# First heads by selecting matmuls, values in column tiles, and all first loads on one queue

## Chip, cores and metric

The kernel runs on one NeuronCore of a Trainium2 chip. The metric is the device time of one execution in microseconds; the time before is the median of three runs, 556.89 us (555.47 to 558.24).

The engines are named as in the profile: PE is TensorE (PEld its weight loads), DVE is VectorE, ACT is ScalarE, POOL is GpSimd and SP is SyncE, which here only issues DMAs.

## What is computed

Four layers in turn on x of 2048 rows and 640 features: attention with a memory, a feed-forward layer, and both once more with the same weights. Cut to what matters:

```python
def _A_ref(x, wq, wk, wv, wo, beta):
    H, Dh, N, L = 32, 20, 4, 512
    q, k, v = ...            # (x @ w), by head, in N segments of L rows
    phi = lambda t: jnp.where(t > 0, t + 1.0, jnp.exp(t))
    g = _sigmoid(beta).reshape(1, H, 1, 1)
    M, z = 0, 0
    for s in range(N):
        p = _softmax(qs @ ks.T * scale + causal_mask)
        a_dot = p @ vs
        a_mem = (phi(qs) @ M) / (phi(qs) @ z + 1e-06)
        outs.append(g * a_mem + (1.0 - g) * a_dot)
        M = M + phi(ks).T @ vs
        z = z + phi(ks).sum(rows)
    return o @ wo

def _B_ref(x, w1, w2):       # 640 -> 1728 -> 640
    return jnp.maximum(x @ w1, 0) @ w2

x = x + _A_ref(_layernorm(x), wq, wk, wv, wo, beta)
x = x + _B_ref(_layernorm(x), w1, w2)
x = x + _A_ref(_layernorm(x), wq, wk, wv, wo, beta)
x = x + _B_ref(_layernorm(x), w1, w2)
```

All arrays are bfloat16; sums are kept in float32.

## The kernel before

**Tiling and staging.** x stays in SBUF as 16 tiles of 128 rows (`x_sb`). A segment has 512 rows, four tiles; the work goes through eight pairs (a, s): layer pair a = 0, 1, segment s = 0 to 3. For each, the rows are normalised, transposed (`xnT`, or parts of `hT` for the early segments), and q, k (features on partitions, five column blocks c of 128, in `stg`) and v (rows on partitions, `v_aug`) are projected. Heads have 20 features. Scores want four heads on the four quarters of the 128 partitions, at 32 hh; so q and k are brought from the dense layout of `stg` into a buffer `pad`, which holds a pair of head groups z = 0, 1 (a group is four heads) for q and k. As a rule this goes through DRAM: `spill` writes a block of `stg` to `scr`, `fill` reads it back head by head, both on SP's queue.

**Scores, exponentials and values.** For each pair of groups there are five rounds of scores (`scores`, row tiles of PE), ten exponentials of 128 x 1024 on ACT into `PT` (`exps`), causal masks on POOL, and then for each group the product with the values (`apply`). There are two forms of it. `apply_by_token` makes rows the partitions: 40 matmuls with weights from `PT` and 21 columns each, and then the division from PSUM by three DVE instructions into `o_sb` (lines 1360 to 1364). The other form, at line 1308, makes four heads four column tiles of PE: 16 matmuls of 512 to 128 columns; the result, features on partitions, is copied to `otu` (line 1318, DVE or ACT), a pair is transposed by a DMA on SP's queue into `otk` (`turn_pair`), and divided by DVE (`divide`, lines 1394 to 1402). `otu` has one buffer. `BY_TOKEN = G` = 8: all eight groups of segment 0 of the first layer go by token, the other 56 by column tiles.

**The opening.** `loads` issues x tiles 0 and 1 on SP's queue, tiles 2 and 3 and beta on ACT's, and then on SP's the first 256 columns of k's and q's weights, the other 384 of each, v's weights and the four x tiles of segment 1. `warm_pe` gives PE 41 matmuls of 128 columns meanwhile. `first_sums` takes the statistics of tiles 0 and 1 on DVE; `first_ln_b` those of tiles 2 and 3 on ACT, by sums and squares; `first_tile` normalises each tile and transposes it on PE. `proj_first` projects blocks 0 and 1 of k and q for the first half of the rows, then for the second, and then blocks 2 to 4 for all rows. `first_heads` fills the first pair's `pad` straight from `stg` by nine DMAs, on SP's queue for z = 0 and ACT's for z = 1.

**What sets the order.** The program is written as streams of operations. `Sched.run` places one operation after another on its engine, by an own estimate of when it can start, plus offsets written out by hand in `SHIFT` (for stream and layer segment) and a priority; the resulting order of each engine is fixed in the program, and so are the semaphores to wait for. The constants there (`lat`, `issue`, nanoseconds of an instruction) serve this order alone. In `evac` either ACT or DVE is taken, whichever the estimate finds earlier. PE works in one of three modes, full, row tiles (scores) or column tiles; matmuls with an alternative by `either` follow the mode that PE is in. From the end of segment 0's first projections until its last scores, two of the four PSUM banks of `MISC` are lent to the scores. `late_loads` brings the remaining x tiles and weights piece by piece, each piece after a set round of exponentials. `proj_ln` normalises later segments; segment 2 of the first layer has a gate of its own there, the scores of pair 2, round 3.

## Time and profile before

| | |
|---|---|
| median of three runs | 556.89 us |
| lowest, highest | 555.47, 558.24 us |
| span of the profiled execution | 554.2 us |
| mean granted TensorE clock | 0.997 |
| DMA packets, bytes | 130307, 61.56 MB |
| exponentials on ACT | 320, 308.7 us |

The span goes from the first to the last instruction of one profiled execution; that execution's own time is not among the runs, which lie 2.7 us above the span at the median. In the profile's rows, L695 is line 695 of the kernel, `ps<-xnT,wk_r` reads "ps is written from xnT and wk_r", `x5` counts instructions, and after a bar stand busy time, the mean in ns, and the idle time of the engine before them with what ended it. A row of the timeline has start and length in us first; a row of the chain of waits has them too. Matmuls overlap one another, so the length of a merged row holds the last one's tail, while the chain counts to the next piece of work. A Q behind an engine's name (SPq) stands for its queue issuing, not for an engine at work.

### The profile page before, as it was taken

How to read it: one execution, taken by the hardware profiler on the slowest of the kernel's cores; microseconds unless marked ns; L12 is line 12 of the kernel's file. 1: busy time of each engine (PE TensorE's matmuls, PEld its weight loads, DVE VectorE, ACT ScalarE, POOL GpSimd, SP SyncE). 2: the span in 40 equal slices, each digit the busy share in tenths (PEclk: the TensorE clock that was granted, in tenths of full speed). 3: DMA queues.
4: the chain of work that ended last, by engine and by line, in shares of the span. 5: the costliest groups of instructions: out<-in, count | busy, mean ns of one | idle time of the engine just before them, and what ended most of it. 6: DMA issues, size and time to landing. Idle time of an engine off the chain costs nothing.

```text
span 554.2 us, 22754 instructions
## 1 busy us (share of the span) xinstructions
PE 544.5 (98%) x10170; PEld 312.7 (56%) x10170; DVE 416.2 (75%) x1051; ACT 410.8 (74%) x526; POOL 191.1 (34%) x303
## 2 busy tenths in 40 slices
PE   7999999999999999999999999999999999999997
PEld 6555554445654664655456565555546645647656
DVE  4877989988798978877788857888978578725302
ACT  4699789999669878877988858889885588661140
POOL 3445444333344334432433404434432243310000
PEclk8999999999999999999999999999999999999999
DMA  8596889835551434893463444548126713213401
GB/s 238 143 237 169 210 183 223 233 92 96 126 102 46 93 67 89 176 119 64 135 143 71 69 70 131 102 97 126 33 40 110 206 43 60 65 39 56 88 2 51
DMA packets 130307, 61.56 MB, mean 111 GB/s; under 512 B 109090, under 2 KB 120098, under 8 KB 130210
## 3 DMA queue, kind: packets, MB, share of 16 engines
q1 hardware_dynamic: 129504, 59.57, 49.5%
q8 instruction: 80, 1.31, 1.0%
q10 hardware_dynamic: 706, 0.54, 0.5%
q14 instruction: 17, 0.14, 0.1%
HBM read 20.57 MB, written 12.85 MB: 60 GB/s over the span
## 4 chain that ended last, share of the span: by engine, by line
PE 82%; DVE 8%; ACT 5%; DMA 3%; SPq 1%; issue 0%
PE ps L695 43%; PE ps L692 21%; PE ps L1214 8%; PE ps L1308 5%; ACT PT L1276 4%; PE ps L1094 2%; DVE stg L894 2%; DMA x_sb<-in_A_x_dram 1%; DVE stats L713 1%; DMA otk<-otu 1%; DVE xn_tok L759 1%; PE ps L1151 1%; DVE phs L1060 1%; PE ps L1488 1%; SPq L551 1%; DVE x_sb L1430 1%
## 5 line engine op out<-in xcount | busy, mean ns | idle before, releaser
L1276 ACT ACTIVATE PT<-ps 128x1024 bf16<-128x1024 f32 x320 | 308.7, 1032 | 63.8 <-PE ps L1214 62.2
L1288 POOL TENSOR_SCALAR_AFFINE_SELECT PT<-PT 128x512 bf16<-128x512 bf16 x256 | 165.6, 664 | 256.5 <-ACT PT L1276 256.5
L695 PE MATMUL ps<-xnT,w_r 128*32 128x512 bf16 x1872 | 115.0, 380 | 0.0
L695 PEld LDWEIGHTS ps<-xnT,w_r 128*32 128x32 bf16 x1872 | 46.0, 96 | 43.6 <-issue 6.1
L695 PE MATMUL ps<-w_r,hT 128*32 128x320 bf16 (+1 forms) x1788 | 67.1, 295 | 0.0
L1214 PE MATMUL ps<-pad 20*128 20x512 bf16 (+3 forms) x1024 | 63.4, 301 | 2.0 <-ACT PT L1276 1.5
L692 PE MATMUL ps<-w_r,hT 128*128 128x320 bf16 x398 | 63.2, 300 | 0.0
L1534 DVE TENSOR_TENSOR x_sb<-x_sb,ps 128x320 bf16<-128x320 bf16 (+1 forms) x65 | 31.0, 478 | 42.2 <-PE ps L695 31.5
L713 DVE BATCH_NORM_STATS2 stats<-x_sb 128x6 f32<-128x320 bf16 x124 | 55.1, 476 | 3.2 <-DMA x_sb<-in_A_x_dram 2.3
L695 PEld LDWEIGHTS ps<-w_r,hT 128*32 128x32 bf16 x1788 | 45.9, 97 | 11.7
L1214 PEld LDWEIGHTS ps<-pad 20*128 20x128 bf16 x1024 | 17.8, 92 | 54.6 <-ACT PT L1276 27.1
L692 PEld LDWEIGHTS ps<-w_r,hT 128*128 128x128 bf16 x398 | 37.0, 98 | 18.3 <-issue 4.4
L1430 DVE TENSOR_TENSOR x_sb<-x_sb,ps 128x320 bf16<-128x320 bf16 x64 | 30.2, 479 | 20.3 <-PE ps L695 13.6
L1512 DVE TENSOR_SCALAR hT<-ps 128x512 bf16<-128x512 f32 x57 | 38.8, 683 | 6.7 <-PE ps L695 5.9
L729 POOL TENSOR_TENSOR rstd<-lnU,mhalf 128x2 f32<-128x2 f32 (+2 forms) x26 | 20.5, 787 | 57.9 <-DVE lnU L725 57.2
L1308 PE MATMUL ps<-PT,v_aug 128*21 128x128 bf16 (+3 forms) x896 | 40.3, 300 | 0.0
L1513 ACT ACTIVATE hT<-ps 128x512 bf16<-128x512 f32 x47 | 28.0, 599 | 13.1 <-PE ps L695 13.0
L1059 ACT ACTIVATE stg<-stg 128x512 bf16<-128x512 bf16 x50 | 31.8, 636 | 5.3 <-DVE rtmp L1057 4.7
L759 DVE TENSOR_SCALAR xn_tok<-x_sb,mv,rstd 128x640 bf16<-128x640 bf16 x60 | 30.4, 538 | 4.0 <-POOL rstd L729 4.0
L695 PE MATMUL ps<-wo_r,oT 128*32 128x320 bf16 x808 | 33.2, 300 | 0.1
L1402 DVE TENSOR_TENSOR o_sb<-otk,rden 128x320 bf16<-128x320 bf16 x56 | 31.3, 587 | 1.1 <-DMA oT<-o_sb 0.7
L1318 DVE CAST otu<-ps 128x512 bf16<-128x512 f32 x40 | 27.3, 682 | 6.3 <-PE ps L1308 6.0
(110 smaller groups left out, 706.1 us busy)
## 6 DMA issues: line engine op xcount, KB each, us to landing
pad<-scr SPq DMA_DIRECT2D x124, 80.0 KB
scr<-stg SPq DMA_DIRECT2D x34, 256.0 KB, 2.5
out_dram<-x_sb SPq DMA_DIRECT2D x15, 160.0 KB, 2.1
w_r<-in_B_w_dram SPq DMA_DIRECT2D x10, 216.0 KB, 2.7
w_r<-in_B_w_dram SPq DMA_DIRECT2D x13, 160.0 KB, 2.9
x_sb<-in_A_x_dram SPq DMA_DIRECT2D x10, 160.0 KB, 2.7
scr<-w_r SPq DMA_DIRECT2D x5, 256.0 KB, 3.1
wv_r<-in_A_wv_dram SPq DMA_DIRECT2D x1, 800.0 KB, 10.1
```

The source lines that it names most:

```text
L692: return e.matmul(view(dst.ap, b), a, b, start=(k == 0), stop=(k == last))
L695: return e.matmul(view(dst.ap[rows], b), part, b, start=(k == 0), stop=(k == last))
L713: tk = yield dve(320, 1, lambda e, c2=c2: e.bn_stats(stats6[:, t, c2, :], x_sb[:, t, c2 * 320:(c2 + 1) * 320]), xt)
L759: nm = lambda e, bx, t, k: e.tensor_scalar(bx.ap[:, k * D:k * D + D], x_sb[:, t + k, :], mv[:, t + k, 0:1], rstd[:, t + k:t + k + 1], ALU. ...
L1059: te = yield act(512, lambda e, q=q: e.activation(q, q, ACT.Exp), [tr] + p, psum=False)
L1214: fns.append([(lambda e, z=z, j=j, hh=hh, N=N, o=o, sl=sl, q=hh % 2: e.matmul(slot.ap[:, q, o:o + N], sl.ap[32 * hh:32 * hh + DH, z, 0, 12 ...
L1276: tx = yield act(1024, lambda e, dst=dst, src=src: e.activation(dst, src, ACT.Exp, scale=SCALE), sc + pw)
L1288: tm = yield pool(600.0, lambda e, reg=reg: e.affine_select(out=reg, in_=reg, pattern=[[0, 4], [1, 128]], compare_op=ALU.is_ge, fill=0.0, ...
L1308: fns.append((lambda e, OD, j=j, hh=hh: e.matmul(OD.ap[32 * hh:32 * hh + DH + 1, 128 * j:L], VAUG[vx(a, s)][:, j, 4 * g + hh, :], pt.ap[:, ...
L1402: to = yield dve(320, 1, lambda e, z=z, dst=dst: e.tensor_tensor(dst, av[:, z, :, :, 0:DH], rd.ap[:, z].to_broadcast([128, NJ, 4, DH]), AL ...
L1430: ta = yield dve(320, 1, lambda e: e.tensor_tensor(x_sb[:, t, 320 * hf:320 * hf + 320], x_sb[:, t, 320 * hf:320 * hf + 320], bk.ap[:, 0:32 ...
L1512: th = yield evac(512, 1, lambda e: e.tensor_scalar(hT[:, dc, :], bk.ap[:, :], 0.0, None, ALU.max), lambda e: e.activation(hT[:, dc, :], b ...
```

## The change

- **Loads.** All first loads go on SP's queue in this order: x tiles 0 and 1, all of k's weights in one DMA, x tiles 2 and 3, all of q's, all of v's, segment 1's x tiles, beta. Six loads get estimates of their own in `LAND`.
- **Statistics.** Tiles 2 and 3 get theirs on DVE, as tiles 0 and 1 do.
- **Order of the first projections.** All five blocks of k for the first half of the rows, all five of q, then the second half: blocks 0 and 1 of k and q, then 2 to 4.
- **Warm-up and filling.** Of the 41 warming matmuls, four get 512 columns and 25 keep 128; after tile 1's transposes PE gets 14 more of 128 columns (`FILL`).
- **First heads.** Three 0/1 matrices `sel` are made on POOL in a spare part of `om_sb`, between the identity and `mhalf`; the first pair's `pad` is filled by six matmuls with them and four copies from PSUM, in place of the nine DMAs.
- **Values.** `BY_TOKEN = (6, G)`: groups 0 to 5 of the first segment go by column tiles, groups 6 and 7 by token.
- **Order.** The matmuls of a group after its first are urgent, segment 2's gate is gone, and `SHIFT` is another table. The changes in `run` only spare the planner from looking at ended streams.

```diff
-BY_TOKEN = G
+BY_TOKEN = (6, G)
+FILL = 14
...
+LAND = {"x000": 1550.0, "x001": 1600.0, "x010": 2900.0, "x011": 2900.0, "wk": 2900.0, "wq": 2600.0, "wv": 2400.0}
...
 SHIFT = {
-    (2, 0): 500, (5, 0): -1500, (7, 0): -3000, (7, 1): 3000, (7, 6): 1500, (8, 1): -700, (8, 2): -100, (8, 4): -100,
...
+    (1, 0): 150, (2, 0): 750, (5, 0): -500, (7, 1): 950, (8, 1): -850, (8, 2): -700, (9, 3): -400, (9, 4): -750,
...
-def pe(ns, fns, waits=(), acq=None, take=(), mode="full", lag=0.0):
-    return Op([("pe", ns, fns, 190.0)], waits, acq=acq, take=take, mode=mode, lag=lag)
+def pe(ns, fns, waits=(), acq=None, take=(), mode="full", lag=0.0, urgent=False):
+    return Op([("pe", ns, fns, 190.0)], waits, acq=acq, take=take, mode=mode, lag=lag, urgent=urgent)
...
         ident = om_sb[:, 0, 0:128]
+        sel = om_sb[:, 0, 128:512].rearrange("p (z n) -> p z n", z=3)
...
-            for t in range(4):
-                yield from ld(("sp", "act")[t // 2], "x0%d%d" % divmod(t, 2), 163840, lambda e, t=t: e.dma_start(
-                    x_sb[:, t, :], xs[:, t, :]))
-            yield from ld("act", "beta", 16384, lambda e: e.dma_start(
-                beta_bc[:], bass.AP(tensor=A_beta.tensor, offset=A_beta.offset, ap=[[0, 128], [1, H]])))
-            yield from cols("wk0", wk_r, A_wk, 0, 256)
-            yield from cols("wq0", wq_r, A_wq, 0, 256)
-            yield from cols("wk1", wk_r, A_wk, 256, D)
-            yield from cols("wq1", wq_r, A_wq, 256, D)
+            def x_one(t):
+                yield from ld("sp", "x0%d%d" % divmod(t, 2), 163840, lambda e: e.dma_start(x_sb[:, t, :], xs[:, t, :]))
+
+            for t in range(2):
+                yield from x_one(t)
+            yield from wload("sp", "wk", wk_r, A_wk)
+            for t in range(2, 4):
+                yield from x_one(t)
+            yield from wload("sp", "wq", wq_r, A_wq)
             yield from wload("sp", "wv", wv_r, A_wv)
             yield from x_pair("x10", 4)
             yield from x_pair("x11", 6)
+            yield from ld("sp", "beta", 16384, lambda e: e.dma_start(
+                beta_bc[:], bass.AP(tensor=A_beta.tensor, offset=A_beta.offset, ap=[[0, 128], [1, H]])))
...
             S.set("ident", tks=[t1])
+            t2 = yield pool(250, lambda e: e.memset(sel, 0.0))
+            tz = []
+            for z, base in enumerate((0, -80, 48)):
+                tz.append((yield pool(250, lambda e, z=z, base=base: e.affine_select(
+                    out=sel[:, z, :].rearrange("p (h j) -> p h j", h=4), in_=sel[:, z, :].rearrange("p (h j) -> p h j", h=4),
+                    compare_op=ALU.not_equal, fill=1.0, base=base,
+                    pattern=[[-DH, 4], [-1, 32]], channel_multiplier=1), [t2])))
+            S.set("sel", tks=tz)
...
-            tw = yield dve(128, 1, lambda e: e.memset(warm_w, 1.0))
+            tw = yield dve(L, 1, lambda e: e.memset(warm_r, 1.0))
             yield Acq([X])
-            tk = yield pe(107.0 * 41, [(warm_mm, k == 40) for k in range(41)], [tw])
+            fns = [(lambda e, k=k: e.matmul(ps[:, 4 + k, :], warm_w, warm_r, start=True, stop=True), False) for k in range(4)]
+            tk = yield pe(107.0 * 41, fns + [(warm_mm, k == 24) for k in range(25)], [tw])
...
-                    tk = yield either(pe(mm_ns(n), fns, w), cols)
+                    tk = yield either(pe(mm_ns(n), fns, w, urgent=True), cols)
...
+            if t == 1:
+                yield pe(56.0 * FILL, [(warm_mm, k == FILL - 1) for k in range(FILL)])
...
         def first_ln_b():
...
-                tk = yield act(D + 130, lambda e, t=t: e.activation(
-                    junk[:, (t - 2) * D:(t - 1) * D], x_sb[:, t, :], ACT.Copy, accum_out=asum[:, t - 2:t - 1]), w, psum=False)
+                tk = yield from stats(t, w)
...
-            if (a, s) == (0, 2):
-                yield Need("sc",2,3,1)
...
-            order = [(c, n, h) for h in range(2) for c in range(2) for n in range(2)]
-            order += [(c, n, None) for c in range(2, FC) for n in range(2)]
+            order = [(c, n, 0) for n in range(2) for c in range(FC)]
+            order += [(c, n, 1) for cs in ((0, 1), (2, 3, 4)) for c in cs for n in range(2)]
...
         def first_heads():
 
             sl = yield Acq(PAD)
-            sems = pad_sem[id(sl)], sem_("first")
+            st = yield Need("sel")
             tks = []
             for z in range(2):
-                ev = []
+                got = []
                 for n in range(2):
-                    t = yield Need("stg", 0, 0, 0, n)
-                    ev = ev + t
...
+                    ev = []
+                    for c in range(z + 1):
+                        t = yield Need("stg", 0, 0, c, n)
+                        ev = ev + t
+                    fns = [(lambda e, bk, c=c, z=z, n=n: e.matmul(
+                        bk.ap[:, :], sel[:, z + c, :], stg[:, c, n, :], start=(c == 0), stop=(c == z)), c == z)
+                        for c in range(z + 1)]
+                    bk, tk = yield pe(mm_ns(L) * (z + 1), fns, ev + st, acq=MISC)
+                    dst = sl.ap[:, z, n, :]
+                    te = yield evac(L, 1, lambda e, bk=bk, dst=dst: e.tensor_copy(dst, bk.ap),
+                                    lambda e, bk=bk, dst=dst: e.activation(dst, bk.ap, ACT.Copy), [tk] + sl.tks)
+                    bk.release(te)
+                    got.append(te)
+                    tks.append(tk)
+                S.set("pad", 0, 0, z, tks=[sl] + got)
             S.set("direct", 0, tks=tks)
-            S.set("direct", 1, tks=tks[1:])
+            S.set("direct", 1, tks=tks[2:])
...
-            if n < BY_TOKEN:
+            if BY_TOKEN[0] <= n < BY_TOKEN[1]:
                 yield from apply_by_token(n, a, s, g, pt, mk + vt)
                 return
```

`turn_pair` and `divide` get the same condition, so that they now also serve the pairs of groups 0 to 5.

More of the change, by code (lines that the diff above doesn't have):

```diff
@@ L203, in __init__ @@
         self.landed = set()
+        self.done = 0
+        self.seen = 0
+        self.live = []
     def add(self, prio, gen):
@@ L316, in run @@
                 moved = False
[L317 to L318 removed]
+                for n, st in enumerate(self.streams[self.done:], self.done):
+                    if st[4] or isinstance(st[2], (Op, Either)):
+                        continue
+                    had = st[2]
                     self._settle(st)
[L320 to L321 removed]
+                    moved = moved or st[4] or st[2] is not had
+            while self.done < len(self.streams) and self.streams[self.done][4]:
+                self.done += 1
             heads = []
[L323 to L324 removed]
+            live = [(n, st) for n, st in self.live if not st[4]]
+            live += list(enumerate(self.streams[self.seen:], self.seen))
+            self.seen = len(self.streams)
+            self.live = [(n, st) for n, st in live if not st[4]]
+            self.soon = min([max([self.at(t) for t in st[2].waits], default=0.0) for n, st in self.live
+                             if isinstance(st[2], Op) and st[2].mode == "cols" and st[2].cols is None],
                             default=1e12)
[L326 to L328 removed]
+            for n, st in self.live:
                 if isinstance(st[2], Op):
@@ L536, in ld @@
         def ld(e, name, nbytes, fn, waits=()):
[L537 removed]
+            tk = yield dma(e, sem_("d_" + name), nbytes, fn, waits, lat=LAND.get(name, 2000.0))
             S.set(name, tks=[tk])
```

43 lines of the change are left out of this document (4 added, 39 removed), and 16 rows, old and new, of the table SHIFT.

## The prediction

> **What bounds the kernel now.** I read the page first, then the busy time by stage, then the opening microseconds as a timeline, then the chain of waits.
>
> ```profile
> span 554.2 us, 22754 instructions
> PE 544.5 (98%) x10170; PEld 312.7 (56%) x10170; DVE 416.2 (75%) x1051; ACT 410.8 (74%) x526; POOL 191.1 (34%) x303
> PE 82%; DVE 8%; ACT 5%; DMA 3%; SPq 1%; issue 0%
> ```
>
> TensorE (PE) is busy for 544.5 of 554.2 us and carries 82% of the chain that ended last. So a microsecond counts where TensorE starts earlier, has less to do, or stops standing idle. The profiled span is 554.2; the median of the runs is 556.89, that is 2.7 more, which I take as a constant around the span. The sum below is made on the span and carried over to the median.
>
> ```profile
> 1.00:4.00 3.00, 2.88 (x28) 2.88 (x29) 0.94 (x4) 1.62 (x3) 0.34 (x3) 1.00 0.67 198
> 4.00:7.00 3.00, 2.63 (x28) 2.19 (x27) 2.21 (x8) 0.49 (x2) 1.70 (x4) 1.00 0.84 160
> 7.00:15.00 8.00, 5.53 (x45) 4.33 (x44) 2.79 (x7) 4.54 (x12) 3.40 (x9) 0.79 0.99 325
> 9.00:10.00 1.00, 0.18 (x2) 0.15 (x3) 0.00 (x0) 1.00 (x3) 0.00 (x0) 0.72 1.03 339
> 10.00:13.00 3.00, 3.00 (x21) 2.20 (x20) 1.12 (x3) 1.02 (x4) 1.63 (x3) 0.52 0.99 317
> 20.00:30.00 10.00, 10.00 (x91) 4.85 (x89) 10.00 (x29) 8.22 (x11) 4.32 (x6) 1.00 0.74 173
> 30.00:40.00 10.00, 9.70 (x143) 5.85 (x140) 7.66 (x18) 9.55 (x12) 3.81 (x7) 1.00 0.96 232
> 40.00:50.00 10.00, 9.74 (x146) 4.88 (x148) 6.55 (x18) 10.00 (x12) 5.85 (x10) 1.00 0.68 199
> 50.00:60.00 10.00, 8.71 (x139) 4.19 (x139) 8.84 (x27) 10.00 (x12) 6.49 (x10) 1.00 0.64 168
> 80.00:100.00 20.00, 19.83 (x330) 9.25 (x322) 19.28 (x47) 18.67 (x24) 7.63 (x13) 1.00 0.88 197
> ```
>
> Each row has the stage, its length, then the busy time of PE, PEld, DVE, ACT and POOL, then the granted clock, the DMA share and GB/s. Three things are to be seen. From 10 to 13 us TensorE works at a clock of 0.52. From 30 to 60 ScalarE is full (9.55, 10.00, 10.00) and TensorE has 0.30 + 0.26 + 1.29 = 1.85 us idle. In the twenties and from 80 to 100 VectorE is full too (10.00 of 10, 19.28 of 20).
>
> ```profile
> 1.24 0.29 POOL L611 TENSOR_SCALAR_AFFINE_SELECT om_sb<-om_sb 128x128 bf16<-128x128 bf16 x1 [0.24 <-POOL om_sb L610]
> 4.35 0.19 POOL L723 TENSOR_SCALAR lnU<-mv 128x1 f32<-128x1 f32 x1 [2.77 <-DVE mv L715]
> 6.14 0.44 PE L663 MATMUL ps<-PT 128*128 128x128 bf16 x5
> 6.76 1.12 DVE L793 COPY xnT<-ps 128x640 bf16<-128x640 bf16 x2
> 6.90 0.45 PE L784 MATMUL ps<-om_sb,xn_tok 128*128 128x128 bf16 x5 [0.31 <-DVE xn_tok L771]
> 9.82 1.22 PE L692 MATMUL ps<-xnT,wk_r 128*128 128x256 bf16 x5 [2.47 <-DMA wk_r<-in_A_wk_dram]
> 11.35 0.80 DVE L771 TENSOR_SCALAR xn_tok<-x_sb,mv,rstd 128x640 bf16<-128x640 bf16 x2 [3.47 <-POOL rstd L729]
> 14.02 0.71 PE L692 MATMUL ps<-xnT,wk_r 128*128 128x256 bf16 x5
> 14.56 0.71 PE L692 MATMUL ps<-xnT,wq_r 128*128 128x256 bf16 x5
> 15.72 3.19 SPq L1010 DMA_DIRECT2D pad<-stg  x4
> 20.95 1.02 ACT L1276 ACTIVATE PT<-ps 128x1024 bf16<-128x1024 f32 x1 [2.03 <-PE ps L1214]
> 9.33 7.25 DMA x_sb<-in_A_x_dram
> 37.92 19.34 ACT PT L1276 x21
> ```
>
> The first half of the normed rows lies transposed at 7.88 (6.76 + 1.12), yet the first projection waits 2.47 us for k's first columns, until 9.82, and meets the slowed clock. POOL stands idle 2.77 us before the first square root. The first exponential starts at 20.95, 5.2 us after the copies that place the heads begin at 15.72. The last two rows are the chain's: the next x tiles land at 16.58 (9.33 + 7.25), and 21 exponentials in a row (37.92 to 57.26) set the pace later.
>
> **The change, part by part. Loads on one queue.** Before k is whole there are now two x tiles and k: 160 + 160 + 800 KB, 1.15 MB. By 4.0 us 3 x 198 = 594 KB have moved; the remaining 0.55 MB take 1.7 us at the 325 GB/s of 7 to 15, or 3.5 us at the 160 of 4 to 7. So k lands at 5.7 to 7.5, as an estimate; the other bound is the 9.82 at which k's first columns came. I take the earlier side, for fewer bytes lie ahead. Then not k but the 14 filling matmuls after the second tile's transposes (7.35) set the start: five took 0.44, of which 0.17 is the last one's tail (a half group below lasts 0.71 and the next one starts after 0.54), so one takes 0.054 to 0.088 and 14 end at 8.1 to 8.6; I take 8.2. Start: 9.82 to 8.2, **-1.6** (bounds -1.9 by the copy's 7.88, and 0).
>
> **Clock.** From 9.82 to 13 the lost share is 0.18 x 0.28 + 3 x 0.48, about 1.5 us. With the fill TensorE stands idle hardly at all before k, so **-1.5**; if k comes so late that the clock drops again, 0. The warm-up is 4 x 512 + 25 x 128 columns for 41 x 128: the same.
>
> **Order of the projections.** Halves cost 0.54 us a group (14.02 to 14.56). beta goes last on the queue, behind all 3.77 MB: (3.77 - 0.59) / 0.325 after 4.0, 13.8; like the x tiles, which landed at 16.58, nothing. Five k groups end at 10.9. q is whole after 2.29 MB: (2.29 - 0.59) / 0.325 after 4.0 is 9.2, with the slow stretch 10.8: hidden, +1.3 if its last packets straggle as k's first columns do. The second half's statistics move from ScalarE to VectorE, which stands idle 3.47 us before 11.35. Tiles 2 and 3 land by 6.7 to 8.2 by the same sum; VectorE's work on them, at the rows below 2 x (2 x 0.476 + 0.203) = 2.3 us, ends at 10.5, and then come the square root on POOL, the normalisation (0.80) and the copies (0.5 each), about 13.6: when the ten first-half groups end (8.2 + 5.4). So nothing, +2.3 if that cover is gone. The 0/1 matrices put a memset and three selects on POOL ahead of the constant that the first square root needs, 4 x 0.29 = 1.2 us by the identity's row: hidden in POOL's 2.77 idle, and 1.2 late if they are not.
>
> **First heads.** Nine DMAs go from the queues of SP (3.19 us of issuing) and ACT. Six 512-column matmuls come, at twice the half group's fifth, 6 x 0.216, **+1.3** (alone, up to 0.39 each: +2.3), and four evictions of 0.682 or less. The first exponential moves from 20.95 to about 16.8: 13.6, two half groups (1.1), an eviction (0.4), selects (0.6), eviction (0.7), scores (0.4).
>
> **Values in column tiles**, heads groups 0 to 5 of segment 0.
>
> ```profile
> 36.54 0.99 PE ps L1347 x40
> 106.81 0.54 PE ps L1308 x16
> 112.05 0.65 PE ps L1308 x16
> 41.25 1.18 PE L1347 MATMUL ps<-w_r,PT 128*128 128x21 bf16 x40
> L1360 DVE RECIPROCAL rden<-ps 128x16 f32<-128x16 f32 x8 | 2.0, 249 | 2.8 <-PE ps L1347 2.8
> L1361 DVE TENSOR_TENSOR rden<-rden,omg 128x16 f32<-128x16 f32 x8 | 1.7, 207 | 0.1
> L1364 DVE TENSOR_TENSOR o_sb<-ps,rden 128x320 bf16<-128x320 f32 x8 | 3.9, 484 | 0.1
> L1318 DVE CAST otu<-ps 128x512 bf16<-128x512 f32 x40 | 27.3, 682 | 6.3 <-PE ps L1308 6.0
> L1394 DVE RECIPROCAL rden<-otk 128x32 f32<-128x32 bf16 x28 | 9.3, 333 | 15.6 <-DMA otk<-otu 15.5
> L1397 DVE TENSOR_TENSOR rden<-rden,omg 128x32 f32<-128x32 f32 x28 | 7.0, 250 | 0.4
> L1402 DVE TENSOR_TENSOR o_sb<-otk,rden 128x320 bf16<-128x320 bf16 x56 | 31.3, 587 | 1.1 <-DMA oT<-o_sb 0.7
> L713 DVE BATCH_NORM_STATS2 stats<-x_sb 128x6 f32<-128x320 bf16 x124 | 55.1, 476 | 3.2 <-DMA x_sb<-in_A_x_dram 2.3
> L715 DVE BATCH_NORM_AGGREGATE mv<-stats 128x2 f32<-128x12 f32 x62 | 12.6, 203 | 1.0
> DMA to landing us min/median/max: 3.0/3.3/5.9
> ```
>
> On TensorE a group falls from 0.99 to about 0.6 on the chain: 6 x 0.39 = -2.3 (bounds -2.7 and 0). Half of it falls where ScalarE sets the pace, so I take **-1.2**. The Trainium skill, TensorEngine Tiling, section Tiling Modes (Key Properties), speaks against this: changing the tiling mode drains TensorE. An estimate of a drain from this case is that tail of 0.17; two drains for each of six groups would be +2.0, and the sum below would be worse by half of that, 553.1. The two rows of 16 matmuls, for 1280 columns in four tiles, lie 0.11 apart, so the trace shows at most that much of it; the sum goes by the rows.
>
> VectorE pays 0.682 x 2 + 0.333 + 0.250 + 2 x 0.587 = 3.12 a pair, for 2 x (0.249 + 0.207 + 0.484) = 1.88: +1.24, three times 3.7 us. In 20 to 60 it has 0 + 2.34 + 3.45 + 1.16 = 6.95 us idle, so I cost it at nothing; uncovered, 3.7. Three transposes join SP's queue, and behind one that waits for its eviction stand the spills and fills of the coming heads and the weight loads; there is a single buffer for a pair, held until its transpose lands, 3.3 us, at most 5.9. Between the end of one pair (36.54 + 0.99) and the next pair's first group (41.25 + 0.99) lie 4.7 us, 4.0 without the eviction: nothing at the median, +1.9 for each of two hand-overs at the maximum.
>
> **Freed order.** The gate that held segment 2's normalisation until pair 2's scores is gone, matmuls within a group are not parted by others, and the hand-tuned offsets are new. With scores up to 4.1 us earlier and segment 2 ready to fill, I count the idle 1.85 of 30 to 60 as won: **-1.8** (bounds 0 and the whole 4.1). The new offsets move every later wait; I allow on both sides for one transpose that lands in 5.9 us where another took 3.3 (2.6 us).
>
> Sum: -1.6 - 1.5 + 1.3 - 1.2 - 1.8 = -4.8: span 549.4, time 552.1, by its own terms 548.5 to 555.5.
>
> **The rivals.** *The lead is lost again where VectorE is full* (80 to 100: 19.28 of 20). Earlier scores and ready tiles then wait there; the 3.7 us of added division are paid from the lead: -4.8 + 3.7 = -1.1, 555.8. For it speaks that VectorE is full in the twenties as well; against it the 6.95 idle between.
>
> *VectorE becomes the bound from 20 us on*, the other side. The added divisions (3.7) and, of the four evictions of 0.682, the half that ScalarE doesn't take (1.4) fall on its path: 5.1. Its lead is that of the next x tiles: from 4 to 7 us 3 x (325 - 160) = 495 KB fewer moved than at the later rate, 1.6 us at most if one queue avoids it. So +5.1 - 1.6 = +3.5, 560.4. It decides once less than half of the 6.95 idle can be used, since then what is left of the 5.1 outgrows the 1.6. For it: the chain's wait for the x tiles leads straight into VectorE's full stage. Against: 2.34 and 3.45 idle in the thirties and forties.
>
> *It doesn't do what it says*: k lands no sooner than 9.7. Then the start gives 0.1; TensorE idles 1.5 us, less than the 2.47 after which it was slow, so the clock stays: -0.1 - 1.5 + 1.3 - 1.2 - 1.8 = -3.3, 553.6.
>
> *More than forecast*: the exponentials' 4.1 us and the tiles' 2.3 count in full: -1.6 - 1.5 + 1.3 - 2.3 - 4.1 = -8.2, 548.7.
>
> **How the numbers follow.** Forecast 0.52, lead lost 0.14, VectorE bound 0.18, k no sooner 0.08, more 0.08. No change, which a measurement can't tell, is within 0.5%, 554.1 to 559.7. Faster: 0.47 of the forecast, 0.08, and 0.05 of the late k: 0.60. Same: 0.04 + 0.14 + 0.03 = 0.21. Slower: 0.18 and 0.01: 0.19. The range runs from 546.5 (the large case with some 2 us of order) to 561 (VectorE's case); the forecast's own is 548.5 to 555.5.
>
> **What would show it.** First projection near 8.2 with a clock of 1.00 from 9 to 13; q's first group not waiting; first exponential near 17; otu evictions from the thirties on, with no wait for otk of over 4 us; ScalarE's full stage ending 3 to 5 us earlier; TensorE's idle in 30 to 60 under 1 us; and the same lead at 100 us as at 60. Wrong it would be if the lead at 60 us is there and gone at 100, or if VectorE shows no idle time between 20 and 60.

## The result, and the profile after

| | before | after |
|---|---|---|
| median (10 runs each, same chip) | 556.51 us | 559.31 us |
| lowest, highest | 555.23, 558.87 us | 557.26, 561.01 us |
| span of the profiled execution | 554.2 us | 557.2 us |

The ratio is 1.0044, with a 95% interval of 1.0025 to 1.0063: slower by 0.4%, inside the forecast's range and on the other side of the kernel before than the forecast had it. It is less than the 0.5% that the prediction took for no change, but the whole interval lies above 1.

The page of the changed kernel, its span, its busy times and the shares of its chain of waits:

```profile
span 557.2 us, 22671 instructions
PE 543.8 (98%) x10127; PEld 313.7 (56%) x10127; DVE 423.8 (76%) x1066; ACT 407.3 (73%) x519; POOL 194.0 (35%) x306
PE 74%; DVE 15%; DMA 7%; ACT 1%; SPq 1%; issue 1%; POOL 1%
```

TensorE is busy for 0.7 us less than before (544.5), and the span is 3.0 longer: the chain goes through VectorE and DMAs for 22% of it, where before it was 11%.

The opening of the changed kernel, from its timeline (start, length):

```profile
8.42 2.89 PE L711 MATMUL ps<-xnT,wk_r 128*128 128x256 bf16 x25 [0.40 <-DMA wk_r<-in_A_wk_dram]
11.57 1.25 PE L711 MATMUL ps<-xnT,wq_r 128*128 128x256 bf16 x10 [0.26 <-DMA wq_r<-in_A_wq_dram]
12.66 0.72 PE L803 MATMUL ps<-om_sb,xn_tok 128*128 128x128 bf16 x10
14.85 0.71 PE L711 MATMUL ps<-xnT,wk_r 128*128 128x256 bf16 x5
17.57 0.59 PE L1008 MATMUL ps<-stg,om_sb 128*128 128x512 bf16 x2
18.00 0.30 PE L711 MATMUL ps<-wv_r,xnT 128*128 128x320 bf16 x1
18.82 1.93 ACT L1281 ACTIVATE PT<-ps 128x1024 bf16<-128x1024 f32 x2
```

The first projection starts at 8.42 in place of 9.82, behind a wait of 0.40 for k's weights; q's first group waits 0.26; the transposes of tiles 2 and 3 stand among q's groups, which go on at 13.21; two selecting matmuls take 0.43 (17.57 to 18.00), and the first exponential comes at 18.82 in place of 20.95.

Busy time by stage, after and then before; the columns are those of the prediction's table (PE first, then PEld, DVE, ACT, POOL, the clock, the DMA share and GB/s):

```profile
10.00:13.00 3.00, 2.74 (x29) 2.27 (x28) 1.82 (x6) 1.77 (x6) 0.94 (x2) 1.00 1.06 358
0.00:20.00 20.00, 17.82 (x158) 13.90 (x159) 12.56 (x40) 9.51 (x22) 8.59 (x27) 1.00 0.58 190
20.00:60.00 40.00, 36.09 (x467) 17.74 (x468) 35.41 (x87) 35.95 (x46) 18.74 (x27) 1.00 0.87 209
60.00:100.00 40.00, 38.67 (x557) 20.40 (x550) 37.75 (x97) 36.41 (x46) 19.18 (x28) 1.00 0.96 194
100.00:540.00 440.00, 436.40 (x8476) 249.47 (x8472) 334.07 (x837) 325.18 (x409) 147.44 (x225) 1.00 0.47 94
```

```profile
0.00:20.00 20.00, 16.05 (x132) 12.93 (x133) 10.22 (x32) 9.14 (x22) 7.60 (x24) 0.91 0.69 201
20.00:60.00 40.00, 38.15 (x506) 19.77 (x503) 33.05 (x89) 37.77 (x44) 20.48 (x31) 1.00 0.76 193
60.00:100.00 40.00, 39.83 (x549) 21.43 (x547) 37.25 (x99) 34.17 (x47) 15.11 (x23) 1.00 0.93 206
100.00:540.00 440.00, 439.15 (x8612) 249.43 (x8608) 332.12 (x830) 329.76 (x416) 147.89 (x225) 1.00 0.45 93
```

Subtract PE's busy time from each stage's length, and the account is there:

| TensorE idle | before | after | difference |
|---|---|---|---|
| 0 to 20 us | 3.95 | 2.18 | -1.77 |
| 20 to 60 | 1.85 | 3.91 | +2.06 |
| 60 to 100 | 0.17 | 1.33 | +1.16 |
| 100 to 540 | 0.85 | 3.60 | +2.75 |

From 20 to 540 us TensorE stands idle 5.97 us longer. The span grew by 3.0, so everything else gained 3.0 - 5.97 = -2.97: 1.77 of idle time in the opening, 0.74 of busy time (544.53 to 543.79), and 0.46 behind 540 us, where the last matmul ends 2.84 us ahead of the end before and 2.38 after. Nearly half of the loss falls after 100 us, where both kernels do the same work and only its order differs (and with it which of the `either` matmuls go in column tiles).

What TensorE waited for from 15 us to the end (total us, times, longest), after and then before:

```profile
PE ps L714 <- DMA xnT<-xn_tok: 1.4, 1, 1.4
PE ps L711 <- DMA oT<-o_sb: 1.1, 1, 1.1
PE ps L714 <- DVE w_r L902: 0.9, 1, 0.9
PE ps L1219 <- DMA pad<-scr: 0.8, 1, 0.8
PE ps L711 <- DVE v_aug L957: 0.7, 1, 0.7
PE ps L1313 <- DVE otu L1323: 0.7, 1, 0.7
PE ps L1219 <- DVE w_r L957: 0.6, 1, 0.6
PE ps L714 <- DMA oT<-o_sb: 0.6, 1, 0.6
...
```

```profile
PE ps L1214 <- ACT PT L1276: 1.5, 3, 0.7
PE ps L695 <- DMA xnT<-xn_tok: 0.5, 1, 0.5
...
```

Eight single waits of 0.6 to 1.4 us (four smaller ones are left out), no stall: four for a copy that VectorE makes, three for a transpose of what VectorE wrote, one for a head. Look at what stands in front of the longest, in the changed kernel's timeline:

```profile
309.23 1.97 POOL L1293 TENSOR_SCALAR_AFFINE_SELECT PT<-PT 128x512 bf16<-128x512 bf16 x3
309.31 2.44 DVE L778 TENSOR_SCALAR xn_tok<-x_sb,mv,rstd 128x640 bf16<-128x640 bf16 x4 [1.12 <-POOL rstd L748]
310.75 3.52 SPq L754 DMA_TRANSPOSE xnT<-xn_tok  x2
317.33 1.05 PE L714 MATMUL ps<-xnT,wk_r 128*32 128x512 bf16 x16 [1.37 <-DMA xnT<-xn_tok]
```

Four normalisations take 2.44 us on VectorE while GpSimd does three causal selects. The first two of these rows point at what the later runs test.

Another loss comes earlier. These are the first scores and exponentials of the second pair of head groups, after and then before:

```profile
33.69 0.40 PE L1219 MATMUL ps<-pad 20*128 20x512 bf16 x4 [0.79 <-DMA pad<-scr]
35.47 1.94 ACT L1281 ACTIVATE PT<-ps 128x1024 bf16<-128x1024 f32 x2
```

```profile
33.71 0.40 PE L1214 MATMUL ps<-pad 20*128 20x512 bf16 x4 [0.30 <-DVE stg L894]
34.14 27.70 ACT L1276 ACTIVATE PT<-ps 128x1024 bf16<-128x1024 f32 x30 [0.31 <-PE ps L1214]
```

The first pair's exponentials begin 2.13 us earlier than before, but the second pair's scores begin at the old time: its heads still go through DRAM, and their fills are issued at 28.57, where it was 28.78. Its exponentials begin 1.33 us later than before, since ScalarE's order has an eviction of `v_aug` ahead of them that has to wait for TensorE (34.93 to 35.37). Before, 30 exponentials then follow without a break; now they are broken up, and from 30 to 60 us ScalarE is busy for 27.14 us in place of 29.55.

### The profile page after: what moved, and what is told of

It is laid out like the page before. It is cut to its first block, busy times and chain, and to the rows that moved or that the text cites. A ratio compares the mean times of both kernels' runs of the same rounds, so it can differ in the third digit from the quotient of the medians.

```text
span 557.2 us, 22671 instructions
## 1 busy us (share of the span) xinstructions
PE 543.8 (98%) x10127; PEld 313.7 (56%) x10127; DVE 423.8 (76%) x1066; ACT 407.3 (73%) x519; POOL 194.0 (35%) x306
## 4 chain that ended last, share of the span: by engine, by line
PE 74%; DVE 15%; DMA 7%; ACT 1%; SPq 1%; issue 1%; POOL 1%
PE ps L714 40%; PE ps L711 19%; PE ps L1219 7%; PE ps L1313 5%; DVE xn_tok L778 2%; DMA oT<-o_sb 2%; DMA x_sb<-in_A_x_dram 2%; DVE stats L732 2%; PE ps L1099 2%; DVE hT L1517 1%; DMA phk<-phs 1%; ACT PT L1281 1%; DVE phs L1065 1%; DVE otu L1323 1%; DMA xnT<-xn_tok 1%
## 5 line engine op out<-in xcount | busy, mean ns | idle before, releaser
L1293 POOL TENSOR_SCALAR_AFFINE_SELECT PT<-PT 128x512 bf16<-128x512 bf16 x256 | 167.5, 671 | 264.3 <-ACT PT L1281 264.1
L714 PE MATMUL ps<-xnT,w_r 128*32 128x512 bf16 x1648 | 100.9, 380 | 0.0
L714 PEld LDWEIGHTS ps<-xnT,w_r 128*32 128x32 bf16 x1648 | 40.8, 97 | 39.2 <-issue 6.5
L711 PE MATMUL ps<-w_r,hT 128*128 128x320 bf16 x389 | 61.3, 300 | 0.0
L732 DVE BATCH_NORM_STATS2 stats<-x_sb 128x6 f32<-128x320 bf16 x128 | 57.1, 474 | 3.5 <-DMA x_sb<-in_A_x_dram 3.0
L714 PEld LDWEIGHTS ps<-w_r,hT 128*32 128x32 bf16 x1824 | 46.7, 97 | 13.6 <-issue 2.7
L711 PEld LDWEIGHTS ps<-w_r,hT 128*128 128x128 bf16 x389 | 35.8, 98 | 17.4 <-issue 4.9
L714 PE MATMUL ps<-wo_r,oT 128*32 128x320 bf16 x924 | 37.7, 300 | 0.6 <-DMA oT<-o_sb 0.6
L903 ACT ACTIVATE stg<-ps 128x512 bf16<-128x512 f32 (+1 forms) x41 | 20.9, 510 | 19.5 <-PE ps L711 10.9
L1323 DVE CAST otu<-ps 128x512 bf16<-128x512 f32 x49 | 33.5, 683 | 1.3 <-PE ps L1313 0.8
```

The costliest lines, as they stand in the source:

```text
L711: return e.matmul(view(dst.ap, b), a, b, start=(k == 0), stop=(k == last))
L714: return e.matmul(view(dst.ap[rows], b), part, b, start=(k == 0), stop=(k == last))
L732: tk = yield dve(320, 1, lambda e, c2=c2: e.bn_stats(stats6[:, t, c2, :], x_sb[:, t, c2 * 320:(c2 + 1) * 320]), xt)
L1293: tm = yield pool(600.0, lambda e, reg=reg: e.affine_select(out=reg, in_=reg, pattern=[[0, 4], [1, 128]], compare_op=ALU.is_ge, fill=0.0, ...
L1323: te = yield evac(L, 1, lambda e: e.tensor_copy(dst, OD.ap), lambda e: e.activation(dst, OD.ap, ACT.Copy), [tk] + OTU[0].tks)
```

## The experiments

Ratios are to the kernel before, run beside it on the same chip. The changed kernel itself was run in the first comparison alone; where a later run is set against it, that is by its ratio, 1.0044.

### Undoing single parts

Four kernels from the changed one: values by token again (e1), the gate of segment 2 again (e2), both (e3), both with the offsets of before (e4).

```diff
-BY_TOKEN = (6, G)
+BY_TOKEN = (0, G)
...
+            if (a, s) == (0, 2):
+                yield Need("sc",2,3,1)
```

> The changed kernel, but groups 0 to 5 by token again. Theory V (VectorE is overfilled from 35 to 60 us by the divisions of the column form and by segment 2's normalisation brought forward): 3.7 us of VectorE work go, TensorE's idle time in 40 to 50 falls from 1.84 to under 1 us and the time by 2 us, to about 557. Theory O (the new offsets fit badly, whatever part is there): 559 within 1.5, idle as before. Theory F (the second pair's heads still come through DRAM at the old time, so the early first scores bring nothing): 559 within 1, and pair 1's first exponential still after 34 us.

> The changed kernel with segment 2's gate back. V: the statistics and normalisation of segment 2 (about 6 us of VectorE) leave 33 to 49 us, VectorE in 40 to 50 falls from 9.76 to under 8, the time by 2 us to about 557. O: 559 within 1.5. F: 559 within 1, pair 1's first exponential after 34 us.

> Tokens and gate both back, so that of the change the opening, the first heads by matrices and the new offsets remain. V: the opening's lead is kept, 553 to 555. O: 557 to 560. F: 557 to 559, the lead of 3.8 us at 12 us being gone at 36 us.

> As the one before with the offsets of the kernel before: the opening and the first heads alone. V: 552 to 555, within 1.5 of the one before. O: at least 2 us faster than the one before. F: 556 to 557, as fast as the kernel before, since nothing of the opening reaches the second pair.

Measured: e1 565.19 us (1.0153, 1.0119 to 1.0187), e2 575.28 (1.0325, 1.0297 to 1.0353), e3 564.99 (1.0143, 1.0111 to 1.0174), e4 573.21 (1.0302, 1.0250 to 1.0354). Every one is 5 us or more above the changed kernel, and none of the forecasts holds.

These runs say little of the parts. A part undone gives `Sched.run` another sequence of estimates and so another order of everything behind it, for which the table of offsets was not made. That it is this order, and not the part, that costs 5 us and more is an inference: these runs don't separate the two.

### The order held from outside

To keep the order, each placement of `Sched.run` was recorded as a list for both kernels, and a kernel was made to follow a list; only operations that the list doesn't know were put in by their estimate.

```diff
+            if self.follow:
+                best, forced = self.by_order(heads, best)
...
+    def listed(self, st):
+        key = self.key[id(st[1])]
+        own, shift = OWN.get(key.split(".")[0] if key not in OWN else key, (0, 0))
+        o = self.count[key]
+        if o < own:
+            return None
+        return self.where.get((key, o - shift))
```

> The changed opening alone (first loads on one queue, first heads by matrices, statistics on VectorE); all values by token as before, and every other operation in the order that the kernel before gave it, held by a recorded list. Theory order (the loss comes from the new order of the later operations, not from the changed parts): the clock and load gain of about 3 us less the selects' 1.3 stays, 553 to 555.5 us against 556.5 of before. Theory parts (the changed parts themselves cost it, on VectorE or in later first heads): no faster than before, 556.5 to 559.

> Column tiles for the values of the first segment alone; the opening of before, and every other operation in the order that the kernel before gave it. Theory order: TensorE saves some 1.2 to 2.7 us of value work and VectorE's longer evictions hide: 554 to 556. Theory parts: the column form's longer evictions on a full VectorE cost more than TensorE saves: 557 to 560.

> The whole change (opening, first heads, statistics, column tiles), with every other operation in the order that the kernel before gave it. Theory order: below before and well below the changed kernel's 559.3, 551 to 555. Theory parts: no better than the changed kernel, 558 to 562.

> Nothing of the change: the opening, the first heads by DMA and the values by token of before, but every other operation in the order that the changed kernel gave it. Theory order: slower than before by what the order loses, 560 to 564. Theory parts: within 1 us of before, 555.5 to 557.5, since the parts that cost are gone.

Measured: n1 563.14 us (1.0104, 1.0087 to 1.0121), n2 563.89 (1.0111, 1.0077 to 1.0146), n3 566.90 (1.0173, 1.0131 to 1.0215), n4 574.40 (1.0315, 1.0291 to 1.0340). Neither theory's numbers. The order of before loses with the new parts (n3) and the new order with the old parts (n4): in n4 one matmul waits 10 us for a transpose.

```profile
PE ps L770 <- DMA hT<-xn_tok: 10.0, 1, 10.0
```

As far as these four runs show, an order fits the durations that it was made for. Parts and order cannot be taken apart by exchanging either; what can be changed with both held is the length of a single kind of instruction. The runs from here on (but e11) keep every engine's order as it was.

### Less work on VectorE, and on GpSimd

e5 and e6 (the same in the kernel before) shorten the statistics on VectorE, by leaving out nine tenths of the columns for most tiles; e7 and e8 shorten the causal selects on GpSimd, by leaving out most of the mask.

```diff
-                    stats6[:, t, c2, :], x_sb[:, t, c2 * 320:(c2 + 1) * 320]), xt)
+                    stats6[:, t, c2, :], x_sb[:, t, c2 * 320:c2 * 320 + (32 if t > 3 else 320)]), xt)
...
-                    reg = PT[:, z, :, PT_OFF[j]:PT_OFF[j] + 128]
+                    reg = PT[:, z, :, PT_OFF[j]:PT_OFF[j] + 8]
...
-                        out=reg, in_=reg, pattern=[[0, 4], [1, 128]], compare_op=ALU.is_ge, fill=0.0, base=0,
+                        out=reg, in_=reg, pattern=[[0, 4], [1, 8]], compare_op=ALU.is_ge, fill=0.0, base=0,
```

> The changed kernel with the order of every engine exactly as it was; only the statistics on VectorE of all x tiles but the first four read 32 of the 320 columns of each half (9/10 of the statistics are left out), so that VectorE has some 0.3 us less to do at each of 120 places. Theory VectorE (the new order books VectorE without idle time, so its evictions and the transposes behind it come late and TensorE waits): 555 to 556.5, that is 3 us or more under the changed kernel's 559.3. Theory transfers (heads and transposes land later than the order allows for, whatever VectorE does): 557.5 to 559.

> The same edit in the kernel before, its order exactly kept. Theory VectorE: the order before has idle time on VectorE, so it gains less than 1 us: 555.5 to 556.5. Theory transfers: no gain either, 556 to 557. If it gains as much as the changed kernel does, VectorE does not tell the two kernels apart.

> The changed kernel with its order kept; GpSimd's causal selects touch 8 of the 128 columns (most of the causal mask is left out), so that GpSimd is idle where it ran beside VectorE. Theory VectorE: VectorE's instructions that took 0.2 to 0.4 us longer beside a select run at their usual length; a part of the gain of the light statistics, 556.5 to 558. Theory transfers: 558.5 to 559.5.

> The same edit in the kernel before, its order kept. Theory VectorE: 555.5 to 556.5, a gain of less than in the changed kernel. Theory transfers: 556 to 557.

| | median | ratio | interval |
|---|---|---|---|
| e5, after, light statistics | 557.18 us | 1.0024 | 1.0010 to 1.0037 |
| e6, before, light statistics | 555.46 | 0.9985 | 0.9962 to 1.0009 |
| e7, after, light selects | 552.66 | 0.9939 | 0.9925 to 0.9952 |
| e8, before, light selects | 555.09 | 0.9970 | 0.9957 to 0.9983 |

Light statistics do about the same to both kernels (from 1.0044 to 1.0024, and from 1 to 0.9985). Light selects take 1.05% from the changed kernel and 0.30% from the one before, and turn their sequence round. It is not the amount of VectorE's work: the page of e5 and that of e7 show nearly the same sum of it,

```profile
PE 543.2 (98%) x10126; PEld 314.0 (57%) x10127; DVE 401.9 (72%) x1066; ACT 407.2 (73%) x519; POOL 194.6 (35%) x306
```

```profile
PE 543.0 (98%) x10126; PEld 314.3 (57%) x10127; DVE 400.4 (73%) x1066; ACT 406.5 (74%) x519; POOL 86.1 (16%) x306
```

22 and 23 us off VectorE, with 557.18 and 552.66 us. It is which instructions get shorter. VectorE's groups in the changed kernel, and then in e7 (busy time, mean ns):

```profile
L732 DVE BATCH_NORM_STATS2 stats<-x_sb 128x6 f32<-128x320 bf16 x128 | 57.1, 474 | 3.5 <-DMA x_sb<-in_A_x_dram 3.0
...
L778 DVE TENSOR_SCALAR xn_tok<-x_sb,mv,rstd 128x640 bf16<-128x640 bf16 x60 | 31.5, 558 | 3.2 <-POOL rstd L748 3.0
L1407 DVE TENSOR_TENSOR o_sb<-otk,rden 128x320 bf16<-128x320 bf16 x62 | 31.1, 529 | 0.5
```

```profile
L732 DVE BATCH_NORM_STATS2 stats<-x_sb 128x6 f32<-128x320 bf16 x128 | 57.2, 474 | 3.1 <-DMA x_sb<-in_A_x_dram 2.6
...
L1407 DVE TENSOR_TENSOR o_sb<-otk,rden 128x320 bf16<-128x320 bf16 x62 | 28.5, 486 | 0.5
L778 DVE TENSOR_SCALAR xn_tok<-x_sb,mv,rstd 128x640 bf16<-128x640 bf16 x60 | 24.1, 436 | 3.2 <-POOL rstd L748 3.0
```

The two forms of the division are best seen in the kernel before, where the prediction's rows have them at 587 and 484 ns. With light selects (e8) they are

```profile
L1402 DVE TENSOR_TENSOR o_sb<-otk,rden 128x320 bf16<-128x320 bf16 x56 | 25.5, 484 | 1.4 <-DMA oT<-o_sb 0.9
...
L1364 DVE TENSOR_TENSOR o_sb<-ps,rden 128x320 bf16<-128x320 f32 x8 | 3.9, 486 | 0.1
```

So the normalisation falls (558 to 436), and so does the division with two inputs in SBUF (587 to 484 before, 529 to 486 in the changed kernel). The division that reads PSUM stays (484 and 486), and so do the statistics, which read SBUF, but with one input (474 and 474). The four normalisations of the timeline above take 1.58 us in e7, not 2.44, and of TensorE's waits for VectorE this is the longest left:

```profile
305.05 1.58 DVE L778 TENSOR_SCALAR xn_tok<-x_sb,mv,rstd 128x640 bf16<-128x640 bf16 x4 [1.13 <-POOL rstd L748]
```

```profile
PE ps L1219 <- DVE w_r L957: 0.3, 1, 0.3
```

The wait for the second pair's heads is not among those that go: 0.8 us in the changed kernel, 1.1 in e7.

The Trainium skill, SBUF — State Buffer, section Who interferes with whom, has a rule for this: VectorE and GpSimd share one pair of SBUF ports. A VectorE instruction with two SBUF inputs and a GpSimd instruction that reads SBUF lock each other out, and so do a VectorE instruction in a mode that uses both port pairs and a GpSimd instruction; whichever comes second waits for the whole of the other. The rows agree for the two forms of the division (587 to 484, and 484 to 486). For the normalisation and the statistics it turns on the mode they run in, which no trace here shows.

### Held up, or late?

The light selects shorten two things: how long VectorE is held up, and how long the masked block is in the making. e9 was to part them (a select of 32 columns, then one of 192 into a table that is read no more), e10 to say where the loss falls.

```diff
+                    w = 32 if m > 1 else 128
+                    reg = PT[:, z, :, PT_OFF[j]:PT_OFF[j] + w]
...
+                    if m > 1:
+                        fns.append((lambda e: e.affine_select(
+                            out=gt[:].rearrange("p a h -> p (a h)").bitcast(dt.bfloat16), in_=maskg[:, 0:192],
+                            pattern=[[1, 192]], compare_op=ALU.is_ge, fill=0.0, base=0, channel_multiplier=-1), True))
...
-                    reg = PT[:, z, :, PT_OFF[j]:PT_OFF[j] + 128]
+                    reg = PT[:, z, :, PT_OFF[j]:PT_OFF[j] + (8 if m < 8 else 128)]
```

> The changed kernel, order kept; from the third pair on each causal select handles 32 of its 128 columns (the rest of the mask is left out), and behind it GpSimd does a second select of 192 columns on a table that nobody needs any more. So the result of a select is ready some 0.3 us sooner, while GpSimd is at work for about as long as before. Theory beside (VectorE is held up by any GpSimd work beside it): no gain, 558 to 561. Theory late (it is the lateness of the masked blocks that cost): nearly all of the light selects' gain, 552.5 to 555.

> The changed kernel, order kept; the causal selects are cut to 8 columns for the first segment's eight pairs alone (until some 125 us), whole afterwards. If the lead is lost for good in the first segment, where VectorE is full: all of the gain, 552.5 to 554. If as much is lost later, where the work of both kernels is the same and only its order differs: about half of it, 555 to 557.

e9 took 555.87 us (0.9987, 0.9970 to 1.0005), between the two forecasts, and so decides nothing. GpSimd's and VectorE's groups show why:

```profile
L1301 POOL TENSOR_SCALAR_AFFINE_SELECT gt<-maskg 128x192 bf16<-128x192 bf16 x240 | 89.8, 374 | 0.0
L1297 POOL TENSOR_SCALAR_AFFINE_SELECT PT<-PT 128x128 bf16<-128x128 bf16 x240 | 80.7, 336 | 246.8 <-ACT PT L1281 240.7
...
L778 DVE TENSOR_SCALAR xn_tok<-x_sb,mv,rstd 128x640 bf16<-128x640 bf16 x60 | 25.5, 458 | 3.2 <-POOL rstd L748 3.0
```

GpSimd worked no less than in the changed kernel (89.8 and 80.7 us in these two rows, 167.5 there), in pieces of 374 and 336 ns, but the normalisations shrank from 558 ns to 458 all the same. As it seems, VectorE gets in between the pieces, so that the run cut the hold too. e10 took 555.23 us (0.9992, 0.9980 to 1.0004), about half of the gain of e7. A segment has four pairs of head groups, so its eight pairs (`m < 8`) are the first two segments, and not the first alone as the expectation has it: half of the gain comes up to some 125 us, the other half behind.

If VectorE gets in between, there is a better test, with the whole mask: each select in two pieces (e12, and e13 in the kernel before) or four (e14). The block comes later, the hold gets shorter, and the theories differ in sign.

```diff
+                    regs = [PT[:, z, h:h + 2, PT_OFF[j]:PT_OFF[j] + 128] for h in range(0, 4, 2)]
+                    tm = yield Op([("pool", 600.0, [(lambda e, r=r: e.affine_select(out=r, in_=r, pattern=[[0, 2], [1, 128]],
+                        compare_op=ALU.is_ge, fill=0.0, base=0, channel_multiplier=-1), r is regs[-1]) for r in regs],
+                        60.0)], ex)
```

> The changed kernel, whole and with its order kept; each causal select is done as two, of two heads each, so that VectorE is held up by at most one piece of some 0.4 us at a time, while the block as a whole is ready some 0.15 us later and GpSimd works a quarter more in all. Theory beside: VectorE's long instructions get shorter and the time falls by 1 to 3 us, 556 to 558. Theory late: the blocks are ready later, 560 to 562.

> The same edit in the kernel before, its order kept. Theory beside: the order before has room on VectorE, so within 1 us of it, 555 to 557. Theory late: 556.5 to 559.

> The changed kernel, whole and with its order kept; each causal select is done as four, of one head each: pieces of 0.3 us, the block ready some 0.4 us later, and GpSimd at work for two thirds more. Theory beside: still shorter holds but more of them; between e12 and the changed kernel, 556.5 to 559. Theory late: 562 to 566.

| | median | ratio | interval |
|---|---|---|---|
| e12, after, two pieces | 555.53 us | 0.9985 | 0.9976 to 0.9995 |
| e13, before, two pieces | 556.14 | 0.9997 | 0.9980 to 1.0014 |
| e14, after, four pieces | 558.32 | 1.0036 | 1.0024 to 1.0049 |

e12 is 0.6% faster than the changed kernel, half a microsecond under the range of the theory of the hold and over 4 us under the other's; the kernel before doesn't answer (0.9997, with an interval around 1). VectorE's and GpSimd's groups in e12:

```profile
L778 DVE TENSOR_SCALAR xn_tok<-x_sb,mv,rstd 128x640 bf16<-128x640 bf16 x60 | 26.6, 476 | 3.0 <-POOL rstd L748 2.8
...
L1293 POOL TENSOR_SCALAR_AFFINE_SELECT PT<-PT 128x256 bf16<-128x256 bf16 x512 | 208.8, 439 | 223.7 <-ACT PT L1281 223.5
```

and GpSimd's in the changed kernel:

```profile
L1293 POOL TENSOR_SCALAR_AFFINE_SELECT PT<-PT 128x512 bf16<-128x512 bf16 x256 | 167.5, 671 | 264.3 <-ACT PT L1281 264.1
```

GpSimd is at work longer, 208.8 us against 167.5, and the normalisations take 476 ns in place of 558. Not every instruction gains: the division with two SBUF inputs takes 538 ns in e12, 529 in the changed kernel. VectorE's whole busy time falls all the same, from 423.8 to 416.1 us. With four pieces (e14) TensorE waits for masked blocks, which it does nowhere among its waits in the changed kernel:

```profile
PE ps L1313 <- POOL PT L1293: 2.4, 2, 1.7
```

So both costs are there, and in the changed kernel the hold is the one that counts. e12 computes all that the reference asks for and is the fastest such version here; its lead over the kernel before is 0.15%, and over e13, the kernel before with the same selects, it is not clear of the noise.

### The offsets fitted anew

The changed kernel with another `SHIFT`, fitted to estimates in which VectorE waits for GpSimd and transposes land later.

```diff
 SHIFT = {
-    (1, 0): 150, (2, 0): 750, (5, 0): -500, (7, 1): 950, (8, 1): -850, (8, 2): -700, (9, 3): -400, (9, 4): -750,
...
```

> The changed kernel, its parts whole, with another table of hand-set offsets, fitted so that the waits behind GpSimd's selects and late transposes are counted. Theory order (the parts save some 2 to 4 us, and the order gave it back at waits that it could have avoided): 553.5 to 556.5, below before. Theory parts (the changed parts cost as much as they save): 558 to 561 whatever the order.

It took 557.82 us (1.0048, 1.0023 to 1.0073), between the two forecasts: no gain over the changed kernel's 1.0044. Whether some order holds the changed kernel's whole lead beside whole selects stays open; this one doesn't.

## Why the prediction was wrong

**Loads on one queue: right in size, but not in what sets it.** Forecast was -1.6, with a start at 8.2 when the filling matmuls end, k being estimated to land by 7.5. The first projection starts at 8.42, that is -1.40, and it waits for k: the filling ends at 8.02, and the last 0.40 us are idle time in front of `wk_r`. So k landed some 0.9 us later than its estimate, and that the filling ended near it was luck.

**Clock, first heads, values: about right in sum.** The clock is 1.00 from 10 to 13. Two selecting matmuls take 0.43, so six cost 1.3, as forecast. A group of the first segment holds TensorE for 0.64 to 0.86 us in column tiles, where it was 1.02 to 1.09 by token (start to the next matmul's start). It is 0.64 with more column tiles behind it and 0.65 and 0.66 with row tiles, so a drain of 0.17 at that change of mode doesn't show. The first four terms together were forecast at -3.0; the opening's idle time and TensorE's busy time together fell by 1.77 + 0.74 = 2.51. They can't be read one by one from this, since the filling turns idle time into busy time.

**Order of the projections: a size off.** The second half begins at 14.85, not at 13.6: the start was 0.2 late, q's first group waited 0.26, and the 0.55 us of tile 2's and 3's transposes, which the sum left out, stand among the groups. The first exponential comes at 18.82, not near 16.8. That took half of the 4.1 us by which scores were to come earlier.

**Freed order: the step that failed.** It counted the 1.85 us of idle time from 30 to 60 as won, because scores would come earlier and segment 2 could fill, with 2.6 us either way for one late transpose. Neither part came true. The lead of the first pair's scores doesn't reach the second pair's, which begin at 33.69 where it was 33.71, behind heads that go through DRAM as before; TensorE waits 0.8 us for these, and from 30 to 60 it is idle for 3.29 us, not under 1. And from 20 to 540 us 5.97 us of idle time were added: not one late transpose but eight waits of over half a microsecond, three of them transposes. The bound was for one accident; an order that is new from end to end can be late at every hand-over. e1 to e4 and n1 to n4 show the scale: kernels with a part or an order exchanged lay 6 to 18 us above the kernel before.

**VectorE "costed at nothing": wrong in its ground.** The cover was counted as idle time, 6.95 us, and there was idle time: 40 - 35.41 = 4.59 us from 20 to 60. But TensorE's waits for VectorE in that stretch are 2.6 us (0.9, 0.7, 0.6 and 0.4), where before they were 0.5: idle time elsewhere doesn't help the copy that is late. And what the division adds are instructions on two SBUF inputs, which are held up beside selects (529 ns in the changed kernel, 486 in e7), in place of ones that read PSUM, which aren't. The hold was in the rows of before, in `o_sb<-otk,rden` at 587 ns against 484 for `o_sb<-ps,rden`; the prediction took the 587 as a duration and did not ask why the same 320 elements cost 0.1 us more. On the added divisions themselves the hold is small: six of them at 43 ns are 0.26 us, an estimate from these rows. Most of it falls on instructions that both kernels have, the normalisations above all, and e10 shows that half of what short selects give lies behind the first two segments.

**The rivals.** The nearest in mechanism was the lead lost where VectorE is full, at 555.8 us. Of the 2.51 us won, 2.06 are gone by 60 us and the rest by 100. But that rival paid the loss once, from 80 to 100; it began earlier, and it went on to the end. The rival of VectorE as the bound came nearest in time, 560.4, for a reason that e5 speaks against: 22 us less work on VectorE give back 0.2%. That k lands no sooner than 9.7 is refuted by the first row of the opening.

**From the span to the time.** The 2.7 us were taken between one execution's span and the median of others. In the runs on record an execution takes 1.8 us more than its own span at the median, so this added nearly a microsecond too much.

**What is shown and what isn't.** Shown: the opening's gain; the waits; that short selects give the changed kernel 1.05% and the one before 0.30%, after which the changed one is the faster (0.9939 against 0.9970); that the same selects in two pieces give 0.6% to the changed kernel and nothing clear of noise to the other. 0.6% is more than the 0.44% that the changed kernel lost against before. By these runs the holds behind GpSimd turn the change from a small gain into a small loss. They are not the whole of what the forecast lacks: with short selects in both kernels the change is worth 0.3%, where 4.8 us, 0.9%, were forecast. Not shown: why the old order takes the same holds with so little loss (e8 and the division's 587 ns show that it has them). It may be that it leaves room ahead of the waits; e11, whose offsets were fitted to estimates with such waits, brought the new one no gain.

## What to carry to other kernels

Before you count an engine's idle time as cover, ask of each added instruction whether it reads SBUF or PSUM, with how many inputs, and what GpSimd does meanwhile: two forms of the same division have the same number of elements, and in the kernel before they differ by 0.1 us while GpSimd's selects are long, and not when these are short. Where an order is fixed in the program, price a new order by what any re-planning has cost, not by one late transfer, and try a part with the order held: shorten one kind of instruction and leave every queue as it is. And follow an early start to the first thing that doesn't move with it: here the second pair's heads came at the old time. Long GpSimd instructions beside a nearly full VectorE may be worth cutting in two; here cutting them in four was too much.

## What the hardware showed besides

- Work on GpSimd can grow and the kernel get faster: 167.5 us of selects in pieces of 671 ns, 208.8 us in pieces of 439 ns, and 0.6% less in the end.
- VectorE's rows overlap. In the changed kernel's timeline

```profile
47.66 0.68 DVE L1323 CAST otu<-ps 128x512 bf16<-128x512 f32 x1
48.26 0.48 DVE L1407 TENSOR_TENSOR o_sb<-otk,rden 128x320 bf16<-128x320 bf16 x1
48.66 0.75 DVE L778 TENSOR_SCALAR xn_tok<-x_sb,mv,rstd 128x640 bf16<-128x640 bf16 x1
```

the copy of 0.68 us lets the next start after 0.60, and the division of 0.48 after 0.40. The prediction's 3.12 us a pair were lengths, by these rows some 0.08 us too much for each instruction that has another right behind it.
